# Attention output for four heads at once in column tiles of 32, and V of batch 0 begun in halves

## Chip, cores, metric

The kernel runs on one core of one Trainium2 chip. The metric is device time in microseconds of one execution. One execution is also taken by the hardware profiler, and the profile and trace below are of that one.

## What is computed

Two networks stand one behind the other. The first is attention in blocks, 4 batches of 8 heads, 768 positions in 8 blocks of 96, head size 64. A small matrix per head (8 x 8) is made doubly stochastic in five rounds; with it the blocks of K and V are mixed, and every block of Q attends to its mixed block. The second is a gated MLP with a spatial gate over the 512 columns that the heads give together.

```
for _ in range(5):
    P = exp(P - max(P)); P = P / sum(P, -1); P = P / sum(P, -2)
k_sorted = einsum('bhij,bhjcd->bhicd', P, k_b)      # the same for v
scores = scale * q_b @ k_sb.T                        # per block, 96 x 96
attn = exp(scores - max); attn = attn / sum(attn)
x = (attn @ v_sb) as (B, S, H * D)
h = relu(x @ w_in); u, v = halves of h
v_n = (v - mean) / sqrt(var + 1e-6)
v_s = w_spatial @ v_n + b_spatial
out = (u * v_s) @ w_out
```

## The kernel before

The work is cut into units, and the order of the units on TensorE, VectorE, ScalarE and GpSimd is written out by hand in one string, SCHEDULE. A unit such as `a41-2` reads: kind `a`, number 4, batch 1, no engine for the copy, PSUM slot 2; `A` and `D` name ScalarE and VectorE for the copy out of PSUM. There are four PSUM slots (tiles ps0 to ps3), each of two banks, so a unit waits until the unit that held its slot before has been read out. Every engine takes its instructions in the order in which the units stand.

The kinds are these. `k` and `q` mix and transpose K, and transpose Q (L288, L276; q unit n gives head pairs 2n and 2n+1); `v` mixes V (L246), which then goes through DRAM (vm to vd to vb, issued on SP's queue) to change its layout; for batch 0 units `t` and `B` do that with transposes instead (L288, L315). `s` makes scores of a pair of heads and half of the blocks, with one exponential on ScalarE (L331, L338). `a` (attend) makes the attention output of a pair of heads and four blocks: eight matmuls of 96 columns (L352), which write 64 partitions for each head, two matmuls with a matrix of ones for the sums of the exponentials (L359), and a Ln on ScalarE (L365). `d` (divide) ends it with an Exp of -1 times the Ln (L371) and a multiply on VectorE (L375) into xt, the transposed input of the MLP. Unit n of `s`, `a` and `d` stands for head pair n // 2 and half n % 2 of the blocks, so each batch has eight of each.

Of the MLP, `V` is the second half of the first projection with its statistics (L393, relu L227, bn_stats L407), three units a batch; `N` the normalization (L413 to L418); `U` the first half (L428); `S` the spatial product (L443) with an add on VectorE (L454) and a product with u on GpSimd (L455; on VectorE in the last batch); `O` the last projection (L465) and the store. `w` transposes w_spatial once. V, N, U, S, O of one batch are interleaved with the attention of the next.

Ahead of the units stands the sinkhorn loop on ScalarE and VectorE. Its result p_bf (32 rows of batch and head) is brought to all partitions by `spread_t` (eight matmuls, a copy) and `spread` (a matmul with a selector, a copy to prep_sb), and `make_pdiag` multiplies it with a mask. For batch 0 that is done at once; for the other three it stands in the string as `P` and `R`, just before V of batch 0, with the products on GpSimd.

Loads of q, k, v and the weights, with a cast, are issued on GpSimd's queue. Loads of batch b+2 are issued when the first S unit of batch b comes up, behind two one-element copies on GpSimd (gate, L537), which read vb of batch b+1 and so wait for its way through DRAM.

Of the kernel before, what the change touches and what calls it, by code (L numbers as in the profile page):

```python
# [8 lines left out]
FP32 = mybir.dt.float32  # L9
# [7 lines left out]
def _raw_ap(base_ap: bass.AP, off_delta: int, dims) -> bass.AP:  # L17
    return bass.AP(
        tensor=base_ap.tensor,
        offset=base_ap.offset + off_delta,  # L20
        ap=[list(d) for d in dims],
    )

# [6 lines left out]
def kernel(  # L30
# [12 lines left out]
    nc = tc.nc  # L43
# [22 lines left out]
    ex_pool = ctx.enter_context(tc.tile_pool(name="ex", bufs=7))  # L66
    xt_pool = ctx.enter_context(tc.tile_pool(name="xt", bufs=8))
    ln_pool = ctx.enter_context(tc.tile_pool(name="ln", bufs=4))
    moe_pool = ctx.enter_context(tc.tile_pool(name="moe", bufs=4))
    vs_pool = ctx.enter_context(tc.tile_pool(name="vs", bufs=2))  # L70
# [20 lines left out]
    def load_heads(x, b, name):  # L91
# [21 lines left out]
    sel16 = const.tile([8, 128], BF16)  # L113
    nc.gpsimd.memset(sel16, 0.0)
    nc.gpsimd.affine_select(
        out=sel16.rearrange("p (j t) -> p j t", t=TB),
        in_=sel16.rearrange("p (j t) -> p j t", t=TB),
        pattern=[[1, NB], [0, TB]], compare_op=ALU.not_equal,
# [6 lines left out]
    ones = const.tile([BLK, D], BF16)  # L125
# [4 lines left out]
    nc.gpsimd.dma_start(out=w_in_sb, in_=moe_w_in.rearrange("(kc p) f -> p kc f", p=128))  # L130
# [42 lines left out]


    pts = {}

    def spread_t(b, nb, ps):
        n = nb * NB * H
        t = ps_tile(ps)
        for i in range(NB):  # L180
            nc.tensor.matmul(
                t[0:NB, 0, 0:n].rearrange("p (b i h) -> p b i h", i=NB, h=H)[:, :, i, :],
                lhsT=p_bf[:, i, :], rhs=ident_bf[0:BH, b * H:(b + nb) * H],
                start=True, stop=True,
            )
        pts[b] = small.tile([NB, B * NB * H], BF16, name="pt", tag="pt", bufs=2)
        nc.vector.tensor_copy(out=pts[b][:, 0:n], in_=t[0:NB, 0, 0:n])

    def spread(b, nb, ps):
        n = nb * NB * H  # L190
        t = ps_tile(ps)
        nc.tensor.matmul(t[:, 0, 0:n], lhsT=sel16, rhs=pts[b][:, 0:n], start=True, stop=True)
        nc.vector.tensor_copy(
            out=prep_sb[:, b:b + nb].rearrange("p b i h -> p (b i h)"), in_=t[:, 0, 0:n],
        )

    pdiag = [pd_pool.tile([128, H, NB, TB], BF16, name="pdiag") for _ in range(B)]

    def make_pdiag(b, eng, h0, n):
        eng.tensor_mul(  # L200
            out=pdiag[b][:, h0:h0 + n],
            in0=_raw_ap(mask16, 0, [mask16.ap[0], [0, n], [TB, NB], [1, TB]]),
            in1=_raw_ap(prep_sb, b * NB * H + h0, [prep_sb.ap[0], [1, n], [H, NB], [0, TB]]),
        )
# [29 lines left out]
    class Attention:  # L234
        def __init__(self, b):
# [4 lines left out]
            self.xt, self.vb, self.acc, self.mixed = {}, None, {}, []  # L240
# [105 lines left out]
        def attend(self, n, eng, ps):  # L346
            hp, ih = n // 2, n % 2
            t = ps_tile(ps)
            for ii in range(NB // 2):
                for hh in range(2):  # L350
                    h, i = 2 * hp + hh, ih * (NB // 2) + ii
                    nc.tensor.matmul(  # L352
                        t[hh * 64:hh * 64 + 64, 0, ii * BLK:(ii + 1) * BLK],
                        lhsT=self.vb[:, i, h // (H // 2), h % (H // 2), :],
                        rhs=self.e[n][:, hh, ii, :],
                        start=True, stop=True,
                    )
            for hh in range(2):
                nc.tensor.matmul(  # L359
                    t[hh * 64:hh * 64 + 64, 1, 0:HW], lhsT=ones,  # L360
                    rhs=self.e[n][:, hh].rearrange("p i c -> p (i c)"),
                    start=True, stop=True,
                )
            lns = ln_pool.tile([128, HW], FP32, name="lns", tag="lns")
            nc.scalar.activation(out=lns, in_=t[:, 1, 0:HW], func=AF.Ln)  # L365
            self.acc[n] = t, lns

        def divide(self, n, eng, ps):
            hp, ih = n // 2, n % 2
            t, lns = self.acc[n]  # L370
            nc.scalar.activation(out=lns, in_=lns, func=AF.Exp, scale=-1.0)  # L371
            if hp not in self.xt:
                self.xt[hp] = xts[self.b, hp] = xt_pool.tile([128, S], BF16, name="xt", tag="xt")
            i0 = ih * (NB // 2)
            nc.vector.tensor_mul(  # L375
                out=self.xt[hp].rearrange("p (g i t) -> p i g t", g=G, i=NB)[:, i0:i0 + NB // 2],
                in0=t[:, 0, 0:HW].rearrange("p (i g t) -> p i g t", g=G, t=TB),
                in1=lns.rearrange("p (i g t) -> p i g t", g=G, t=TB),
            )


    class Gmlp:
        def __init__(self, b):
            self.b, self.last = b, b == B - 1
            self.v, self.u, self.gt, self.mv = {}, {}, {}, None
            self.xt = [xts[b, kc] for kc in range(KC)]

        def vproj(self, n, eng, ps):
            t = ps_tile(ps)
            for x in range(2):  # L390
                g = 2 * n + x
                for kc in range(KC):
                    nc.tensor.matmul(  # L393
                        t[:, x, :], lhsT=self.xt[kc][:, g * 128:(g + 1) * 128],
# [182 lines left out]
```

The softmax here doesn't subtract the row's maximum and nothing guards it: scores larger than these inputs give would overflow.

## Time and profile before

| | |
|---|---|
| median of 4 runs | 167.25 us (164.66 to 168.71) |
| the profiled execution | 168.69 us, span from first to last instruction 166.9 us |
| mean granted TensorE clock in it | 0.969 |
| TensorE matmuls busy | 152.3 us |
| ScalarE busy | 109.9 us |
| VectorE busy | 97.3 us |
| GpSimd busy | 43.1 us |
| Ln, 32 of 128 x 384 (L365) | 14.4 us, 486 ns each |
| Exp of the divide, 32 of 128 x 384 (L371) | 15.7 us, 526 ns each |
| multiply into xt, 32 of 128 x 384 (L375) | 16.9 us, 554 ns each |

Busy time of a row is the time in which at least one of its instructions is under way. Matmuls overlap one another, so their mean duration (209 ns for the eight of an attend unit) says little of what one costs; the chain of waits counts only what each adds. In the row of the granted clock (PEclk) each of the 40 digits stands for 4.2 us, 9 for full clock and 5 for half.

### The profile page before, as it was taken

Reading aid. Unit: us, or ns where it says so; the run is one execution under the profiler, and the core shown is the slowest. Engines: PE = TensorE matmul, PEld = TensorE weight load, DVE = VectorE, ACT = ScalarE, POOL = GpSimd, SP = SyncE. Lnnn points to the kernel's source line nnn. Section 1 sums busy time; section 2 is a strip of 40 time slices with the busy share of each in tenths; the row PEclk is TensorE's granted clock in tenths of the full one; section 3 lists DMA queues with packets and bytes.
Section 4 is the critical chain, followed back from the end, with each engine's and each line's share of the span. In section 5 each row is a group of like instructions: output and inputs, shape, how many; then the busy total and the mean of one; then the engine's idle time right before and its main releaser. Section 6 shows DMA issues by size and latency. Waiting matters only on the chain.

```text
span 166.9 us, 3916 instructions
## 1 busy us (share of the span) xinstructions
PE 152.3 (91%) x1645; PEld 88.2 (53%) x1645; DVE 97.3 (58%) x203; ACT 109.9 (66%) x181; POOL 43.1 (26%) x46
## 2 busy tenths in 40 slices
PE   0979996999999999999996999999999999999880
PEld 0266863546856554457663454458655544565330
DVE  4667887158971552389222255788242658849951
ACT  3168997368877777689956496489959964560041
POOL 7931000970029560000059230000163300000000
PEclk9999997599999999999999599999999999999999
DMA  2999999999657997605529993616400036000045
GB/s 15 198 204 209 231 255 186 205 204 228 221 127 95 202 204 198 251 7 168 171 46 175 204 177 132 251 57 198 126 4 0 4 132 251 0 0 4 0 184 193
DMA packets 21554, 23.86 MB, mean 143 GB/s; under 512 B 736, under 2 KB 18144, under 8 KB 21408
## 3 DMA queue, kind: packets, MB, share of 16 engines
q0 software_dynamic: 13760, 12.58, 47.1%
q1 hardware_dynamic: 7776, 11.02, 18.5%
q8 instruction: 13, 0.21, 0.5%
q14 instruction: 5, 0.04, 0.1%
HBM read 27.14 MB, written 8.65 MB: 214 GB/s over the span
## 4 chain that ended last, share of the span: by engine, by line
PE 64%; DVE 11%; ACT 10%; DMA 6%; issue 5%; POOL 2%; DVEq 0%; POOLq 0%; SPq 0%
PE ps L393 14%; PE ps L443 13%; PE ps L465 10%; PE ps L428 10%; PE ps L352 4%; ACT ex L338 3%; DVE vs L454 3%; PE ps L331 3%; PE ps L359 2%; DMA vb<-vd 2%; DVE gt L455 2%; PE ps L288 2%; PE ps L246 2%; PE ps L276 2%; PE ps L212 2%
## 5 line engine op out<-in xcount | busy, mean ns | idle before, releaser
L443 PE MATMUL ps<-wspT,v_sb 128*128 128x384 bf16 x192 | 35.1, 338 | 0.0
L338 ACT ACTIVATE ex<-ps 96x768 bf16<-96x768 f32 x32 | 24.3, 806 | 8.7 <-PE ps L331 8.6
L454 DVE TENSOR_TENSOR vs<-ps,b_bc 128x768 f32<-128x768 f32 (+1 forms) x20 | 15.9, 795 | 23.2 <-PE ps L443 18.2
L455 POOL TENSOR_TENSOR gt<-vs,u_sb 128x768 bf16<-128x768 f32 x12 | 19.7, 1653 | 34.4 <-ACT ex L338 31.4
L375 DVE TENSOR_TENSOR xt<-ps,lns 128x384 bf16<-128x384 f32 x32 | 16.9, 554 | 19.7 <-ACT lns L371 19.7
L443 PEld LDWEIGHTS <-v_sb 128*128 128x128 bf16 x192 | 18.3, 101 | 12.8 <-issue 1.9
L393 PE MATMUL ps<-w_in_sb,xt 128*128 128x512 bf16 x96 | 24.3, 407 | 0.0
L465 PE MATMUL ps<-w_out_sb,gt 128*128 128x512 bf16 x96 | 22.2, 380 | 0.8 <-DVE gt L455 0.8
L428 PE MATMUL ps<-xt,w_in_sb 128*128 128x384 bf16 x128 | 22.6, 326 | 0.0
L227 ACT ACTIVATE v_sb<-ps 128x1024 bf16<-128x1024 f32 (+1 forms) x15 | 12.5, 852 | 15.4 <-PE ps L393 15.4
L407 DVE BATCH_NORM_STATS2 stats<-v_sb 128x6 f32<-128x512 bf16 x24 | 16.3, 677 | 10.9 <-ACT v_sb L227 10.8
L428 PEld LDWEIGHTS <-w_in_sb 128*128 128x128 bf16 x128 | 12.2, 98 | 8.1
L221 ACT COPY o_sb<-ps 128x256 f32<-128x256 f32 (+1 forms) x11 | 7.3, 663 | 13.8 <-DVE o_sb L223 12.1
L365 ACT ACTIVATE lns<-ps 128x384 f32<-128x384 f32 x32 | 14.4, 486 | 2.9 <-PE ps L359 2.9
L393 PEld LDWEIGHTS <-xt 128*128 128x128 bf16 x96 | 9.8, 104 | 12.1 <-issue 2.0
L371 ACT ACTIVATE lns<-lns 128x384 f32<-128x384 f32 x32 | 15.7, 526 | 0.2
L465 PEld LDWEIGHTS <-gt 128*128 128x128 bf16 x96 | 8.6, 98 | 12.4 <-DVE gt L455 1.3
L352 PE MATMUL ps<-ex,vb 96*64 96x96 bf16 x256 | 11.3, 209 | 2.5 <-DVE vs L454 1.6
L352 PEld LDWEIGHTS <-vb 96*64 96x64 bf16 x256 | 8.6, 109 | 7.7 <-issue 6.3
L227 ACT ACTIVATE u_sb<-ps 128x768 bf16<-128x768 f32 x13 | 10.3, 809 | 1.7 <-PE ps L428 1.2
L359 PE MATMUL ps<-ex,ones 96*64 96x384 bf16 x64 | 10.8, 326 | 0.0
L221 ACT CAST kT<-ps 128x768 bf16<-128x768 f32 x13 | 10.0, 806 | 1.0 <-PE ps L288 1.0
(73 smaller groups left out, 176.8 us busy)
## 6 DMA issues: line engine op xcount, KB each, us to landing
out_dram<-o_sb SPq DMA_DIRECT2D x9, 512.0 KB, 2.8
q_in<-in_q_dram POOLq DMA_DIRECT2D x4, 768.0 KB, 10.9
k_in<-in_k_dram POOLq DMA_DIRECT2D x4, 768.0 KB, 13.9
v_in<-in_v_dram POOLq DMA_DIRECT2D x4, 768.0 KB, 10.2
vd<-vm SPq DMA_DIRECT2D x6, 384.0 KB, 3.7
vb<-vd SPq DMA_DIRECT2D x6, 384.0 KB, 3.6
out_dram<-o_sb SPq DMA_DIRECT2D x6, 256.0 KB, 2.1
wsp_nat<-in_moe_w_spatial_dram POOLq DMA_DIRECT2D x1, 1152.0 KB, 22.1
```

The costliest lines, as they stand in the source:

```text
L221: nc.scalar.copy(out=out, in_=in_)
L227: nc.scalar.activation(out=out, in_=in_, func=AF.Relu)
L338: nc.scalar.activation(out=e.rearrange("p h i c -> p h (i c)"), in_=t[0:BLK, :, 0:NB // 2 * BLK], func=AF.Exp, scale=scale,)
L352: nc.tensor.matmul(t[hh * 64:hh * 64 + 64, 0, ii * BLK:(ii + 1) * BLK], lhsT=self.vb[:, i, h // (H // 2), h % (H // 2), :], rhs=self.e[n][ ...
L375: nc.vector.tensor_mul(out=self.xt[hp].rearrange("p (g i t) -> p i g t", g=G, i=NB)[:, i0:i0 + NB // 2], in0=t[:, 0, 0:HW].rearrange("p (i ...
L393: nc.tensor.matmul(t[:, x, :], lhsT=self.xt[kc][:, g * 128:(g + 1) * 128], rhs=w_in_sb[:, kc, DH:DFF], start=(kc == 0), stop=(kc == KC - 1),)
L407: nc.vector.bn_stats(out=stats, in_=v_sb[:, x, :])
L428: nc.tensor.matmul(t[:, x, 0:HW], lhsT=w_in_sb[:, kc, mc * 128:(mc + 1) * 128], rhs=self.xt[kc][:, x * HW:(x + 1) * HW], start=(kc == 0), ...
L443: nc.tensor.matmul(t[:, x, 0:HW], lhsT=self.v[g][:, mc * 128:(mc + 1) * 128], rhs=wspT[:, g, x * HW:(x + 1) * HW], start=(g == 0), stop=(g ...
L454: nc.vector.tensor_add(out=vs[:, x], in0=t[:, x, 0:HW], in1=b2[:, x])
L455: eng.tensor_mul(out=gt2[:, x], in0=vs[:, x], in1=u2[:, x])
L465: nc.tensor.matmul(t[:, x, :], lhsT=self.gt[mc][:, g * 128:(g + 1) * 128], rhs=w_out_sb[:, mc, :], start=(mc == 0), stop=(mc == FC - 1),)
```

## The change

Attend units now serve four heads (half j of the heads) and four blocks. The head's 64 columns are taken in two halves dh of 32, and the four heads write the four groups of 32 partitions of one PSUM tile, with a tile position for each: 32 matmuls of 96 columns in a unit, in groups of four heads. The sums get a unit of their own, `z`: four matmuls of 384 columns with a matrix of ones of 32 columns, one Ln, one Exp for the four heads together. The unit `d` is gone; the attend unit ends with two multiplies, one for each dh. xt has one tile for each half of the heads; the rows of w_in are loaded in the order that fits it, in four DMAs instead of one.

Unit `X` does the first half (kc 0 and 1) of a V unit; for batch 0, X10 and X00 stand before U20, and V10 and V00 finish them after it. The order of units is new throughout. p_bf is transposed on VectorE in two pieces of 32 x 32, `spread` does eight matmuls with a selector each, and batch 0's pdiag is made straight from PSUM; the spread of the other batches stands ahead of the first K unit. The gate and the loads of batch b+2 come after the second S unit, in the order v, k, q. In the last batch only the last S unit is done in halves on VectorE; the other three are done as in the other batches, with the product on GpSimd. Buffers: ex 8 for 7, vs 3 for 2, xt 4 of twice the size for 8.

```diff
...
-    ex_pool = ctx.enter_context(tc.tile_pool(name="ex", bufs=7))
-    xt_pool = ctx.enter_context(tc.tile_pool(name="xt", bufs=8))
+    ex_pool = ctx.enter_context(tc.tile_pool(name="ex", bufs=8))
+    xt_pool = ctx.enter_context(tc.tile_pool(name="xt", bufs=4))
     ln_pool = ctx.enter_context(tc.tile_pool(name="ln", bufs=4))
...
-    vs_pool = ctx.enter_context(tc.tile_pool(name="vs", bufs=2))
+    vs_pool = ctx.enter_context(tc.tile_pool(name="vs", bufs=3))
     vsb_pool = ctx.enter_context(tc.tile_pool(name="vsb", bufs=4))
...
-    sel16 = const.tile([8, 128], BF16)
-    nc.gpsimd.memset(sel16, 0.0)
+    sel = const.tile([BH, NB // 2, 128], BF16)
+    nc.gpsimd.memset(sel, 0.0)
     nc.gpsimd.affine_select(
-        out=sel16.rearrange("p (j t) -> p j t", t=TB),
-        in_=sel16.rearrange("p (j t) -> p j t", t=TB),
-        pattern=[[1, NB], [0, TB]], compare_op=ALU.not_equal,
+        out=sel.rearrange("p i (j t) -> p i j t", t=TB),
+        in_=sel.rearrange("p i (j t) -> p i j t", t=TB),
+        pattern=[[NB, NB // 2], [1, NB], [0, TB]], compare_op=ALU.not_equal,
         fill=1.0, base=0, channel_multiplier=-1,
...
-    ones = const.tile([BLK, D], BF16)
+    DQ = D // 2
+    ones = const.tile([BLK, DQ], BF16)
     nc.vector.memset(ones, 1.0)
...
-    nc.gpsimd.dma_start(out=w_in_sb, in_=moe_w_in.rearrange("(kc p) f -> p kc f", p=128))
+    for j in range(2):
+        for dh in range(2):
+            nc.gpsimd.dma_start(
+                out=w_in_sb[:, 2 * j + dh, :],
+                in_=_raw_ap(
+                    moe_w_in, (j * (H // 2) * D + dh * DQ) * DFF,
+                    [[D * DFF, H // 2], [DFF, DQ], [1, DFF]],
+                ),
+            )
     nc.gpsimd.dma_start(out=b_nat, in_=_raw_ap(moe_b_spatial, 0, [[0, 128], [1, S]]))
...
+    pdiag = [pd_pool.tile([128, H, NB, TB], BF16, name="pdiag") for _ in range(B)]
+    def make_pdiag(b, eng, h0, n, src=None):
+        base = h0 if src is not None else b * NB * H + h0
+        src = prep_sb if src is None else src
+        eng.tensor_mul(
+            out=pdiag[b][:, h0:h0 + n],
+            in0=_raw_ap(mask16, 0, [mask16.ap[0], [0, n], [TB, NB], [1, TB]]),
+            in1=_raw_ap(src, base, [src.ap[0], [1, n], [H, NB], [0, TB]]),
+        )
+    p_t = pers.tile([BH, 2, BH], BF16)
+    def transpose_p():
+        for x in range(2):
+            nc.vector.transpose(
+                out=p_t[:, x, :], in_=p_bf[:, x * (NB // 2):(x + 1) * (NB // 2), :].rearrange("p i j -> p (i j)"),
+            )
...
+        if b:
+            nc.tensor.matmul(t[:, 1, :], lhsT=ident_bf, rhs=warm_sb, start=True, stop=True)
+        for i in range(NB):
+            nc.tensor.matmul(
+                t[:, 0, 0:n].rearrange("p (b i h) -> p b i h", i=NB, h=H)[:, :, i, :],
+                lhsT=sel[:, i % (NB // 2), :],
+                rhs=p_t[:, i // (NB // 2), b * H:(b + nb) * H],
+                start=True, stop=True,
+            )
+        if b == 0:
+            for h0, nh in ((0, 2), (2, 2), (4, 4)):
+                make_pdiag(0, DVE, h0, nh, t.rearrange("p x c -> p (x c)"))
+        else:
+            nc.vector.tensor_copy(
+                out=prep_sb[:, b:b + nb].rearrange("p b i h -> p (b i h)"), in_=t[:, 0, 0:n],
+            )
...
-            self.xt, self.vb, self.acc, self.mixed = {}, None, {}, []
+            self.xt, self.vb, self.r, self.mixed = {}, None, {}, []
...
-        def attend(self, n, eng, ps):
-            hp, ih = n // 2, n % 2
+        def sums(self, m, eng, ps):
+            j, ih = m // 2, m % 2
+            t = ps_tile(ps)
+            for c in range(H // 2):
+                nc.tensor.matmul(
+                    t[c * DQ:(c + 1) * DQ, 0, 0:HW], lhsT=ones,
+                    rhs=self.e[4 * j + 2 * (c // 2) + ih][:, c % 2].rearrange("p i c -> p (i c)"),
+                    start=True, stop=True, tile_position=(0, c * DQ),
+                )
+            lns = ln_pool.tile([128, HW], FP32, name="lns", tag="lns")
+            nc.scalar.activation(out=lns, in_=t[:, 0, 0:HW], func=AF.Ln)
+            nc.scalar.activation(out=lns, in_=lns, func=AF.Exp, scale=-1.0)
+            self.r[m] = lns
+        def attend(self, m, eng, ps):
+            j, ih = m // 2, m % 2
             t = ps_tile(ps)
...
+                i = ih * (NB // 2) + ii
+                for dh in range(2):
+                    for c in range(H // 2):
+                        nc.tensor.matmul(
+                            t[c * DQ:(c + 1) * DQ, dh, ii * BLK:(ii + 1) * BLK],
+                            lhsT=self.vb[:, i, j, c, dh * DQ:(dh + 1) * DQ],
+                            rhs=self.e[4 * j + 2 * (c // 2) + ih][:, c % 2, ii, :],
+                            start=True, stop=True, tile_position=(0, c * DQ),
+                        )
+            if j not in self.xt:
+                self.xt[j] = xts[self.b, j] = xt_pool.tile([128, 2, S], BF16, name="xt", tag="xt")
+            i0, r = ih * (NB // 2), self.r[m]
+            for dh in range(2):
+                nc.vector.tensor_mul(
+                    out=self.xt[j][:, dh, :].rearrange(
+                        "p (g i t) -> p i g t", g=G, i=NB)[:, i0:i0 + NB // 2],
+                    in0=t[:, dh, 0:HW].rearrange("p (i g t) -> p i g t", g=G, t=TB),
+                    in1=r.rearrange("p (i g t) -> p i g t", g=G, t=TB),
+                )
...
+            self.vt = {}
+        def xt(self, kc):
+            return xts[self.b, kc // 2][:, kc % 2, :]
+        def vsteps(self, n, ps, kcs):
+            if n not in self.vt:
+                self.vt[n] = ps_tile(ps)
+            for kc in kcs:
+                for x in range(2):
+                    g = 2 * n + x
                     nc.tensor.matmul(
-                        t[:, x, :], lhsT=self.xt[kc][:, g * 128:(g + 1) * 128],
+                        self.vt[n][:, x, :], lhsT=self.xt(kc)[:, g * 128:(g + 1) * 128],
                         rhs=w_in_sb[:, kc, DH:DFF],
...
                     )
+        def vstart(self, n, eng, ps):
+            self.vsteps(n, ps, range(KC // 2))
+        def vproj(self, n, eng, ps):
+            self.vsteps(n, ps, range(KC // 2 if n in self.vt else 0, KC))
+            t = self.vt[n]
             if self.mv is None:
...
-                        rhs=self.xt[kc][:, x * HW:(x + 1) * HW],
+                        rhs=self.xt(kc)[:, x * HW:(x + 1) * HW],
                         start=(kc == 0), stop=(kc == KC - 1),
...
-            if self.last:
+            final = self.last and len(self.gt) == FC - 1
+            if final:
                 pairs = [(g, x) for x in range(2) for g in range(G)]
...
-            for x in (slice(0, 1), slice(1, 2)) if self.last else (slice(0, 2),):
+            for x in (slice(0, 1), slice(1, 2)) if final else (slice(0, 2),):
                 nc.vector.tensor_add(out=vs[:, x], in0=t[:, x, 0:HW], in1=b2[:, x])
...
+        k00A2 k10D3 k20A0 s10-1 s00-2 s30-3 k30D0 t30D1 t00A2 t20D0 s20-3 s50-1 t10D2 s70-0
+        B00D3 s60-1 s40-2 B30D0 B10D3 z00-1 B20D2 z10-0 a00-1 a10-3 z20-2 a20-0 z30-1 a30-2
+        X10-3 X00-1 U20D0 V10-- V00-- w10D2 w30A0 V20-3 v01A1 U10A0 v11A3 v31D2 w00A1 U00D0
+        k01A3 v21D1 w40A2 w20D0 w50D3 k11A1 k21A2 k31A0 q11D3 q01D1 N00-- U30A2 s51-0 s71-3
+        S10-1 s31-2 s01-0 S20-3 s11-1 s21-2 S00-0 z31-3 z01-1 S30-2 s41-3 s61-0 a01-1 z11-2
+        a31-3 a11-0 z21-1 a21-2 O10A3 O00D1 O20D0 V01-2 v32A3 v02D1 V21-0 v22A2 V11-3 v12A0
+        U11A1 k32A2 q12D3 k12A0 q02D1 k02D2 N01-- k22A3 U21A0 s32-1 s22-3 S11-2 s72-0 s42-1
+        S21-3 s52-2 s02-0 U01A1 s62-3 s12-2 U31D0 z02-1 S01-3 z32-2 z12-1 S31-0 z22-2 a32-3
+        a02-1 a22-2 a12-0 O11D3 O01A1 O21A2 V02-0 v33A3 v03D1 V22-2 v23A0 V12-3 v13A2 U12A1
+        k33A0 q13D3 k13A2 q03D1 k03D0 N02-- k23A3 U22A2 s33-1 s23-3 S12-0 s73-2 s43-1 S22-3
+        s53-0 s03-2 U02A1 s63-3 s13-0 U32D2 z03-1 S02-3 z33-0 z13-1 S32-2 z23-0 a33-3 a03-1
+        a23-0 a13-2 O12D3 O02A1 O22A0 V03-2 V13-3 V23-1 N03-- U03A0 U13A2 U23A3 U33A1 S03-0
+        S13-2 S23-3 S33-1 O03A0 O13A2 O23A3
     """
...
-        "v": "vmix", "k": "ktr", "q": "qtr", "s": "score", "a": "attend", "d": "divide",
+        "v": "vmix", "k": "ktr", "q": "qtr", "s": "score", "z": "sums", "a": "attend",
         "t": "vtr", "B": "vblk",
-        "V": "vproj", "N": "norm", "U": "uproj", "S": "spatial", "O": "oproj",
+        "X": "vstart", "V": "vproj", "N": "norm", "U": "uproj", "S": "spatial", "O": "oproj",
     }
...
+        warm(2, 1)
+        transpose_p()
+        spread(0, 1, 0), spread(1, 3, 1)
+        for x in range(1, B):
+            make_pdiag(x, nc.gpsimd, 0, H)
+        nc.gpsimd.tensor_copy(
+            out=b_bc.rearrange("p (g c) -> p g c", g=G),
+            in_=b_nat.rearrange("p (c g) -> p g c", g=G),
+        )
         for step in SCHEDULE.split():
...
+            if name == "w":
                 wsp_unit(n, eng, ps)
-            elif name in "VNUSO":
+            elif name in "XVNUSO":
                 if b not in gmlp:
...
+                    eng = DVE if b == B - 1 and len(gmlp[b].gt) == FC - 1 else nc.gpsimd
                 getattr(gmlp[b], UNITS[name])(n, eng, ps)
+                if name == "S" and b + 2 < B and len(gmlp[b].gt) == 2:
+                    gate = small.tile([1, 2], BF16, name="gate", tag="gate")
+                    for x in range(2):
+                        nc.gpsimd.tensor_copy(
+                            out=gate[:, x:x + 1], in_=attn[b + 1].vb[0:1, 0, x, 0, 0:1],
+                        )
+                    v_in[b + 2] = load_heads(v, b + 2, "v_in")
+                    k_in[b + 2] = load_heads(k, b + 2, "k_in")
+                    q_in[b + 2] = load_heads(q, b + 2, "q_in")
             else:
```

## Prediction

> **What bounds the kernel now.** First the page: engine shares, granted clock by slice, the chain's shares.
>
> ```profile
> PE 152.3 (91%) x1645; PEld 88.2 (53%) x1645; DVE 97.3 (58%) x203; ACT 109.9 (66%) x181; POOL 43.1 (26%) x46
> PEclk9999997599999999999999599999999999999999
> PE 64%; DVE 11%; ACT 10%; DMA 6%; issue 5%; POOL 2%; DVEq 0%; POOLq 0%; SPq 0%
> ```
>
> TensorE is the bound on average, and its clock is halved twice. ScalarE's 66% is worth something only where it leads. So next the chain in order of time:
>
> ```profile
> 22.09 0.41 ACT lns L371
> 22.50 0.39 ACT lns L365
> 22.91 0.52 ACT lns L371
> ...
> 26.46 0.53 ACT lns L371
> 27.01 0.56 DVE xt L375
> 27.57 0.27 DVE pt L187
> 27.88 0.34 PE ps L192
> 28.21 3.52 PE ps L393 x8
> ```
>
> Until 28.2 us batch 0 hangs on ScalarE: score exponentials, then a Ln and an Exp per attention unit. The first eight V matmuls then take 3.52 us; eight later ones take 1.73 (216 ns for 512 columns, 0.42 ns per column). The half rate lasts to about 34. From 28 to 148 TensorE runs without a gap, but for one place in batch 2, in the timelines of GpSimd and TensorE:
>
> ```profile
> 84.83 0.18 POOL L537 COPY gate<-vb 1x1 bf16<-1x1 bf16 x1 [4.32 <-DMA vb<-vd]
> 88.04 4.87 POOL L455 TENSOR_TENSOR gt<-vs,u_sb 128x768 bf16<-128x768 f32 x3
> 90.77 0.36 PE L352 MATMUL ps<-ex,vb 96*64 96x96 bf16 x8 [1.60 <-DVE vs L454]
> 91.87 3.80 PE L443 MATMUL ps<-wspT,v_sb 128*128 128x384 bf16 x12
> ```
>
> GpSimd's gate copies wait for V's trip through DRAM; the gate products stand behind them, the two vs buffers stay full, VectorE waits, TensorE idles 1.6 us. The S unit after it runs at half rate: 3.73 us in the chain where the others take 2.06.
>
> The attention units, from the chain:
>
> ```profile
> 130.46 0.36 PE ps L352 x8
> 130.82 0.16 PE ps L359 x2
> 130.99 1.87 PE ps L465 x8
> 132.86 0.29 PE ps L352 x8
> 133.15 0.16 PE ps L359 x2
> 133.31 0.17 PE ps L352 x8
> ```
>
> Eight matmuls of 96 columns in 0.17 us are 21 ns each, though one streams 96 x 0.42 = 40 ns: the two tiles of 64 columns run side by side. Two sums of 384 columns take 0.16, the time of one. A unit after another kind of matmul pays about 0.12 more (0.29 against 0.17). In batch 3 the eight units took 0.79 + 0.79 + 0.53 + 1.23 = 3.34 us.
>
> The tail, TensorE's timeline and the landing of q_in:
>
> ```profile
> 157.94 4.06 PE L465 MATMUL ps<-w_out_sb,gt 128*128 128x512 bf16 x18 [0.81 <-DVE gt L455]
> DMA to landing us min/median/max: 7.4/10.9/31.4
> ```
>
> In the tail VectorE's eight pairs of add and product pace the end. The 31.4 is q_in of batch 1, issued at 9.1 on GpSimd's queue, landed at 40.5; the loads of that queue land one after the other, 3.9 us for each head tensor (v_in of batch 1 at 32.7, k_in at 36.6).
>
> [...]
>
> **The front (to V of batch 0).** Removed: spread_t, its copy, the second spread with the 0.27 + 0.34 us just before V. Added: two VectorE transposes, eight selector matmuls per spread, pdiag of batch 0 straight from PSUM. p_bf stands at 11.23. Mask copy 0.2; two transposes are unknown: nearest row, a 32x64 multiply at 0.21, so 0.4 (0.3 to 0.8); eight matmuls 0.34 as L181's. First pdiag at about 12.4 instead of 12.60. Three pdiag pieces at L200's prices (0.43, 0.43, 0.69) instead of 0.43 and 0.95, plus the other batches' prep copy 0.35 moved here: the first K copy starts about where it did (13.7).
> ScalarE then: two K copies and the wait between them to 15.5, eight exponentials at 0.70 back to back (2.11 for three), one V copy 0.75, and instead of eight Ln/Exp pairs of 0.9 four: 15.5 + 5.6 + 0.75 + 3.6 = 25.5, where it ended at 28.2. Now VectorE is late next: from 12.4, pdiag 1.55, prep 0.35, five copies of 0.92, four vb copies of 0.67, eight xt multiplies of 0.51 = 13.2, and 1.7 of waiting on slots (the last K copy for ScalarE, B30 for ex70): 27.3. V need not wait for that: X10 takes slot 3, free after the second multiply of a10, the fourth of the eight: about 25.4. X10 and X00, eight matmuls, lie beside the multiplies of a20 and a30; U20's second half finds xt at 27.3. V begins 2.8 us earlier: **-2.8** (0 if VectorE's waits double, -3.5 if transposes cost nothing).
> The half clock costs 2.9 us now (28.2 to 34). [...] Whether that keeps the clock is open: 0 to -2.9. At full clock TensorE reaches q11 at 39.8 and waits for q_in at 40.5, which caps the gain. I take **-1.0**. The same cap holds for v01 (32.5 against 32.7) and k01 (36.5 against 36.6). Splitting w_in into four issues adds about 1.6 us of issuing on GpSimd, and the ninth and later loads wait for older ones, but the queue is backlogged until 43, so nothing lands later. pdiag of batches 1 to 3 moves from 28 to about 20 on GpSimd, covered: v01 reads it after 32.
> In the V stage, w10, v21 and w20 now copy on VectorE behind the bn_stats of three V units; TensorE waits for slots at v21, w20, k11: **+0.7**.
>
> **Attention in batches 1 to 3.** Removed per batch: 3.34 us of units. Added: four sums (z), four tiles of 32 at once, 0.16 each; four attends of 32 matmuls. Four at a time that is 8 x 42 ns = 0.34, as much array time as two old units; three switches at 0.12. Together 0.64 + 1.36 + 0.36 = 2.36: **-1.0 per batch, -3.0 in all**. Not shown: four tiles at once. Bounds: 0.34 (all overlap) and 0.68 (21 ns per matmul, two at a time); I take 0.34, because starts that lie this close show no per-instruction cost.
> ScalarE saves 16 pairs, 16 x (0.486 + 0.526) = 16 us, 12 of them in these batches: off the path, so nothing. VectorE's 32 multiplies stay. But an attend now holds a slot until two multiplies are through, and z needs a slot until its Ln: stepping through the order, I find O11 waiting 0.5 for slot 3 (a32's multiplies behind the add of S31), and 0.1 to 0.3 at z11, a11, a22: **+0.7 per batch, +2.1** (0 to 4).
>
> **The gate.** It moves behind the second S unit; vs has three buffers; all four V mixes come before U. In batch 2 the last mix (v12) is then 10.7 us of TensorE work ahead of the end of S21, plus 2.6 for its add and product; the trip took about 9 (mixed at 75.9, landed at 84.8). So no wait on it: **-1.6 - 1.7 = -3.3** (0 to -3.3). The three loads are issued later: in batch 0 at about 51.5 instead of 49.7. v_in then lands at about 60 and v32 asks at 62.7; k_in before q_in now, at 63.7 and 67.6, asked at 68.1 and 68.5. Covered, by 1 us at the least; if the cover goes, TensorE waits for what is missing.
>
> **The tail.** Three of the four S units go to VectorE's add (0.96) and GpSimd's product (1.65), each under the 2.06 of an S unit. From the start of S03: S23's product on GpSimd ends at 8.9, S33's halves on VectorE at 8.45 and 9.55, so O03 goes on at 9.0 where it now goes on at 157.94 - 147.86 = 10.1: **-1.1** (0 to -1.5).
>
> **Sum.** -2.8 - 1.0 + 0.7 - 3.0 + 2.1 - 3.3 - 1.1 = -8.4 against the profiled execution, 168.7 (span 166.9 and 1.8 around it): **160.3**, with a span of about 158.5. That execution lies 1.4 above the median of 167.25; executions with fewer half-rate windows will stand lower on both sides.
>
> **Rivals.**
> Early gain lost to loads and slots (0.16): q_in on its serial queue and VectorE's longer list take the 3.8 of the front and clock, slots 1 more: about 165. For it: 0.7 us of slack at q_in. Against: U20 and two k units, 2 us, are done before q11 that came after it.
> Four tiles two at a time (0.10): 12 x (0.34 + 0.16) = 6.0 more: 166.3, no change.
> Slower (0.06): tiles of 32 don't overlap. An attend is 32 x 42 = 1.36, a z 0.64: 12 x (1.02 + 0.48) = 18: 178. It decides once an attend and its z take over 0.50 + 8.4/12 = 1.2 us. Against it: the pairs of today.
> Clock kept as well (0.08): no early half-rate window, q_in capping it: about 158.
> My forecast has 0.60, its own range 158 to 163. Measurement of this kernel tells about 2% from no change. Faster 0.79 (forecast, clock kept, and about half of the 165 case whose lower end lies under 163.9), same 0.14, slower 0.07. Range 156.5 to 166, with the two-at-a-time case at its upper edge.
>
> **What would show it.** Right: attend units of 32 matmuls in 0.3 to 0.4 us of chain; V begun at 25 to 26 behind an xt multiply; no idle at the gate and S01 at 2.06; ScalarE near 94 us; O03 resuming 9 us after S03. Wrong: attends of 0.7 or more, TensorE idle at L276 on q_in, GpSimd's gate before a wait of TensorE, or half rate in places where it is full now.

## The result, and the profile after

The changed kernel takes as long as the one before: 167.28 us in the median of 43 runs (164.47 to 170.55) against 165.83 in 64 runs of the kernel before beside them, a ratio of 1.0005 [0.9984, 1.0025]. The forecast of 160.3 lies under every run. Executions of both kernels differ in how much half clock they hold (mean granted clock 0.967 to 1.000 before, 0.949 to 0.989 after); the ratio leaves the longest ones out, but both profiled executions (168.7 and 170.55 us) are among these, so what is read from them is held against the traces of other kernels below.

The page of the changed kernel: engine shares, granted clock by slice, the chain's shares, and the line of queue q8, whose kind it calls "instruction" (packets, MB, share of the DMA engines).

```profile
span 168.8 us, 4366 instructions
PE 148.7 (88%) x1897; PEld 86.4 (51%) x1897; DVE 98.7 (58%) x201; ACT 91.9 (54%) x142; POOL 50.3 (30%) x52
PEclk9999997599999996599999999999999999999997
PE 72%; DMA 8%; DVE 8%; issue 5%; ACT 3%; POOL 2%; POOLq 1%; DVEq 0%
q8 instruction: 15, 0.25, 0.6%
```

TensorE has 3.6 us less to do and ScalarE 18 us less (109.9 to 91.9, foreseen near 94), yet the span is 1.9 us longer: the saved time has become idle time. Half rate has moved: the stretch around 92 is gone, one at 64.7 to 71.5 is new. The chain in order of time shows where the idle time is (start, length, what; "issue" is a wait for nothing that the profile shows):

```profile
24.07 0.68 PE ps L387 x64
24.75 0.17 PE ps L369 x4
24.92 0.08 PE ps L387 x6
25.00 3.59 issue
28.59 0.74 PE ps L387 x25
...
61.80 0.16 PE ps L369 x4
61.96 0.32 PE ps L387 x29
62.27 3.19 issue
65.47 0.27 PE ps L387 x3
65.73 8.15 PE ps L501 x24
```

Two attend units are cut in the middle of their 32 matmuls, for 3.59 and 3.19 us. The profile names no semaphore, slot or load that ends these waits. After the second the clock falls, and the 24 O matmuls take 8.15 us where they take 5.34 in batch 2. There is one more wait in the front, in TensorE's timeline:

```profile
17.74 1.20 PE L307 MATMUL ps<-pdiag,v_in 128*64 128x128 bf16 x36 [1.77 <-DMA v_in<-in_v_dram]
```

v_in of batch 0 landed at 16.3 before and at 17.7 after, and everything behind it on GpSimd's queue of loads (the software queue below) is late: the four pieces of w_in come at 24.9 to 25.6 (22.0 before), v_in of batch 1 at 36.4 (32.7), its q_in at 44.2 (40.5). GpSimd issued this q_in only at 25.2 us (9.1 before), when the first piece of w_in had landed.

Batch 2 and the tail went as worked out:

```profile
99.58 0.28 PE ps L369 x4
99.85 0.71 PE ps L387 x64
100.56 1.02 DVE xt L397 x2
101.58 0.14 issue
101.72 5.34 PE ps L501 x24
...
150.60 5.86 PE ps L479 x36
...
159.37 1.68 PE ps L501 x7
```

Stage by stage, from the first V matmul of a batch (its end is the start of the next):

| stage | before | after | difference | forecast |
|---|---|---|---|---|
| start to end of O of batch 0 | 66.9 | 73.9 | +7.0 | -3.4 |
| attention of batch 2, to the end of O of batch 1 | 37.0 | 33.2 | -3.8 | -3.6 |
| attention of batch 3, to the end of O of batch 2 | 33.7 | 33.2 | -0.5 | -0.3 |
| tail, from V of batch 3 | 29.3 | 28.6 | -0.7 | -1.1 |

(The forecast's first row is front, clock, V stage and the attention of batch 1.) The whole miss, 10.4 us, is in the first row. Three things there that the forecast lacks make 11.4: two stalls 6.8, half rate on O 2.8, the v_in wait 1.8. They are not independent of one another, and the half clock at 27 to 34, which the forecast hoped to shorten, stayed too, so this is no exact account.

### The profile page after: what moved, and what is told of

Read it like the earlier page. It is cut to its first block, busy times and chain, and to the rows that moved or that the text cites. A ratio compares the mean times of both kernels' runs of the same rounds, so it can differ in the third digit from the quotient of the medians.

```text
span 168.8 us, 4366 instructions
## 1 busy us (share of the span) xinstructions
PE 148.7 (88%) x1897; PEld 86.4 (51%) x1897; DVE 98.7 (58%) x201; ACT 91.9 (54%) x142; POOL 50.3 (30%) x52
## 2 busy tenths in 40 slices
DMA packets 23139, 23.89 MB, mean 142 GB/s; under 512 B 2320, under 2 KB 19728, under 8 KB 22992
## 3 DMA queue, kind: packets, MB, share of 16 engines
q0 software_dynamic: 15344, 12.59, 50.0%
## 4 chain that ended last, share of the span: by engine, by line
PE 72%; DMA 8%; DVE 8%; issue 5%; ACT 3%; POOL 2%; POOLq 1%; DVEq 0%
PE ps L479 18%; PE ps L501 14%; PE ps L420 12%; PE ps L463 11%; DMA v_in<-in_v_dram 8%; PE ps L350 4%; PE ps L307 3%; PE ps L387 3%; PE ps L295 2%; DVE stats L442 2%; PE ps L369 2%; ACT ex L357 2%; PE ps L265 2%; DVE xt L397 1%; DVE vm L242 1%
## 5 line engine op out<-in xcount | busy, mean ns | idle before, releaser
L491 POOL TENSOR_TENSOR gt<-vs,u_sb 128x768 bf16<-128x768 f32 x15 | 24.6, 1647 | 94.6 <-ACT ex L357 67.4
L479 PE MATMUL ps<-wspT,v_sb 128*128 128x384 bf16 x192 | 33.4, 327 | 0.0
L501 PE MATMUL ps<-w_out_sb,gt 128*128 128x512 bf16 x96 | 24.4, 415 | 0.9 <-DVE xt L397 0.8
L463 PE MATMUL ps<-xt,w_in_sb 128*128 128x384 bf16 x128 | 23.2, 328 | 0.0
L442 DVE BATCH_NORM_STATS2 stats<-v_sb 128x6 f32<-128x512 bf16 x24 | 16.2, 675 | 11.4 <-ACT v_sb L246 11.4
L240 ACT COPY o_sb<-ps 128x256 f32<-128x256 f32 (+1 forms) x11 | 7.3, 664 | 28.3 <-PE ps L501 16.5
L397 DVE TENSOR_TENSOR xt<-ps,lns 128x384 bf16<-128x384 f32 x32 | 15.5, 549 | 5.8 <-PE ps L387 5.5
L501 PEld LDWEIGHTS <-gt 128*128 128x128 bf16 x96 | 9.7, 105 | 14.2 <-issue 4.9
L420 PEld LDWEIGHTS <-xt 128*128 128x128 bf16 x96 | 9.6, 101 | 11.4 <-issue 1.7
L387 PE MATMUL ps<-ex,vb 96*32 96x96 bf16 x512 | 8.3, 215 | 6.9 <-issue 6.8
L375 ACT ACTIVATE lns<-ps 128x384 f32<-128x384 f32 x16 | 7.8, 485 | 8.2 <-PE ps L369 8.2
L242 DVE COPY o_sb<-ps 128x256 f32<-128x256 f32 (+1 forms) x10 | 7.4, 742 | 7.8 <-PE ps L501 6.4
L387 PEld LDWEIGHTS <-vb 96*32 96x32 bf16 x512 | 7.4, 101 | 7.7 <-issue 7.3
L350 PEld LDWEIGHTS <-kT 64*96 64x96 bf16 x256 | 7.2, 121 | 4.6 <-issue 3.6
```

The lines of the kernel that those rows point to most:

```text
L240: nc.scalar.copy(out=out, in_=in_)
L387: nc.tensor.matmul(t[c * DQ:(c + 1) * DQ, dh, ii * BLK:(ii + 1) * BLK], lhsT=self.vb[:, i, j, c, dh * DQ:(dh + 1) * DQ], rhs=self.e[4 * j ...
L397: nc.vector.tensor_mul(out=self.xt[j][:, dh, :].rearrange("p (g i t) -> p i g t", g=G, i=NB)[:, i0:i0 + NB // 2], in0=t[:, dh, 0:HW].rearr ...
L420: nc.tensor.matmul(self.vt[n][:, x, :], lhsT=self.xt(kc)[:, g * 128:(g + 1) * 128], rhs=w_in_sb[:, kc, DH:DFF], start=(kc == 0), stop=(kc ...
L442: nc.vector.bn_stats(out=stats, in_=v_sb[:, x, :])
L463: nc.tensor.matmul(t[:, x, 0:HW], lhsT=w_in_sb[:, kc, mc * 128:(mc + 1) * 128], rhs=self.xt(kc)[:, x * HW:(x + 1) * HW], start=(kc == 0), ...
```

## The experiments

**Theory F (fetch).** F takes TensorE's instructions to come in blocks, one with each packet of q8, by these counts from the traces: each of q8's packets has 16,384 bytes; 15 of them go with 3806 records of TensorE here (matmuls, weight loads and its few semaphore instructions), 13 with 3298 before, two packets more for 508 records. The stalls stand behind records 705 and 1729, 1024 apart, and those of the runs below behind 705, 961, 1729 and 2753: 256 is the largest number that divides all these distances. So a block is taken as 256 records, an estimate from these counts. New attend code has 64 records in 0.35 us of array time, so it uses up a block in a few microseconds: the block ending at 705 was entered at 20.7 and used up by 25.0. Its successor's packet started only at 26.3, 5.6 us after that entry; the second stall's 3.1 us after. While loads of the software queue run, the other packets of this trace start 2.8 to 3.8 us after the entry; where none run, from 2.4 before it to 1.4 after. So F says: the fetch of the next block waits behind the loads, and fast code reaches the block's end first. Rivals of F: a stall that belongs to the attend code itself (tile positions, slots), and loads that come late by the split of w_in alone. The expectations below name these theories as they stood before each run.

**Shift the code against the blocks** (32 tiny matmuls, 64 instructions, after the warm-up; then 64 of them):

```diff
+    def pad(n, ps):
+        t = ps_tile(ps)
+        for _ in range(n):
+            nc.tensor.matmul(t[0:8, 0, 0:8], lhsT=ident_bf[0:32, 0:8], rhs=warm_sb[0:32, 0:8], start=True, stop=True)
...
+        pad(32, 1)
```

> 32 tiny matmuls (64 instructions with their weight loads, about 0.8 us) are put where TensorE waits for the sinkhorn loop; all other work is as in the changed kernel. Theory F (fetch): TensorE's instructions come in blocks of 256, fetched by DMA, and the two stalls stand where a block ends that was used up before the next had come. Then both stalls move by 64 instructions, 32 matmuls earlier in the order of units: the first from the 7th matmul of a20 to about the 10th of a10, the second from the 30th of a21 to about z21; the first is 2 to 4 us, the second 1.5 to 3. Rival P (place): the stalls belong to the units (a tile mode, a semaphore, a bank of PSUM): they stay in a20 and a21 at 3.6 and 3.2 us. Rival C (clock): the stalls are incidental and the time is lost to half-rate windows alone: no statement on places, time unchanged.

Measured: 165.05, ratio 0.9941 [0.9914, 0.9968], profiled span 162.3. The expectation had both stalls move; they are gone, and no other has come. That fits F, though it was not foreseen: the block that ends at record 705 now lasts 6.4 us, and the block that ends at 1729 has its successor's packet 0.9 us before it is itself entered, ahead of the loads. v_in is waited for longer, 3.48 us.

> As e1_pad64 with 64 tiny matmuls (128 instructions, 1.6 us beside the sinkhorn loop). F: the block ends then fall on the 11th matmul of a00 and on the first matmuls after X10 or V10 in the front, and on a11 in batch 1. The block before a11 then holds an S unit and lasts over 5.5 us, so the second stall is gone or under 1 us and the clock after it stays full: some 4 to 6 us less in the profile, about 164 to 166. In the front one stall of 1 to 4 us remains at one of the two places. P: stalls in a20 and a21 as before, time as the changed kernel.

Measured: 171.13, ratio 1.0324 [1.0191, 1.0457], span 168.8. The expected time, 164 to 166, was missed by far, as were the number and the lengths of the stalls: the second one is gone as expected, but three new ones have come, at block ends in other places. Two of them in TensorE's timeline, the second in a V unit, where no tile of 32 columns is:

```profile
27.92 0.77 PE L395 MATMUL ps<-ex,vb 96*32 96x96 bf16 x54 [1.26 <-issue]
33.88 0.59 PE L428 MATMUL ps<-w_in_sb,xt 128*128 128x512 bf16 x1 [2.83 <-issue]
```

They are at records 705 and 961, both block ends; a third of 1.27 us is in O at 2753, a block end too. v_in is waited for 2.72 us, and half rate holds from 19.8 to 23.2 and from 30.1 to 36.9. The code did not change but by the tiny matmuls at the start, so a stall of the attend code itself is out.

**Take the loads away.** The loads of q, k and v for batches 2 and 3, which run during the second stall, are dropped, and these batches compute on the data of batches 0 and 1; the front is untouched.

```diff
-                    v_in[b + 2] = load_heads(v, b + 2, "v_in")
-                    k_in[b + 2] = load_heads(k, b + 2, "k_in")
-                    q_in[b + 2] = load_heads(q, b + 2, "q_in")
+                    v_in[b + 2], k_in[b + 2], q_in[b + 2] = v_in[b], k_in[b], q_in[b]
```

> The loads of q, k, v for batches 2 and 3 are left out (these batches work on the data of batches 0 and 1); nothing else changes, so block ends stay where they are. F with its second half (a fetch takes 3 to 6 us only because the software queue's loads stand in its way): the first stall stays at 3.6 us, the second goes (under 0.5 us), and so does the half rate after it; 5 to 6 us less in the profile. If a fetch takes that long by itself, the second stall stays at about 3 us. P: both stay.

Measured: 164.15, ratio 0.9898 [0.9808, 0.9988]. Timeline of TensorE at the two places:

```profile
27.77 0.75 PE L387 MATMUL ps<-ex,vb 96*32 96x96 bf16 x26 [3.32 <-issue]
...
60.88 0.53 PE L387 MATMUL ps<-ex,vb 96*32 96x96 bf16 x32
61.59 4.69 PE L501 MATMUL ps<-w_out_sb,gt 128*128 128x512 bf16 x21 [0.18 <-PE ps L387]
```

The first stall stays, the second and its half clock are gone, and the block's packet starts 0.3 us before its entry instead of 3.1 after it. So for the second stall both parts of F are shown: it needs the block's end and the loads. For the first the loads can't be dropped, as the front computes on them; that part is carried over, not shown. The 1% is not the price of the second stall alone: whatever else the loads cost goes with them.

**Load w_in in one DMA again**, the rows paired so that it fits the new order:

```diff
-    for j in range(2):
-        for dh in range(2):
-            nc.gpsimd.dma_start(out=w_in_sb[:, 2 * j + dh, :], in_=_raw_ap(...))
+    nc.gpsimd.dma_start(
+        out=w_in_sb.rearrange("p (j x) f -> p j (x f)", j=2),
+        in_=_raw_ap(moe_w_in, 0, [[2 * DFF, 128], [(H // 2) * D * DFF, 2], [1, 2 * DFF]]),
+    )
...
-                            lhsT=self.vb[:, i, j, c, dh * DQ:(dh + 1) * DQ],
+                            lhsT=self.vb[:, i, j, c, :].rearrange("p (d x) -> p x d", x=2)[:, dh, :],
```

> w_in in one DMA again: even and odd columns of a head instead of first and second half, so that a partition reads two neighbouring rows of 8 KB in all; the attend's weights are then read with a step of two. If the four DMAs with an outer dimension of 4 are what slowed the queue, v_in of batch 0 lands at 16.3 instead of 17.7, w_in at about 22 instead of 25.6, q_in of batch 1 at 40.5 instead of 44.2, and 1.4 us of waiting at t30 go. F: the first stall stays in a20, perhaps shorter, since less stands in the fetch's way; time 1 to 2 us less. If the order of loads on the queue and not the form of the DMA was the cause: nothing changes. If weights with a step of two load slower, attends go from 0.35 to over 0.5 us.

Measured: 164.32, ratio 0.9857 [0.9633, 1.008], by itself unclear. Its timeline isn't:

```profile
16.36 1.36 PE L302 MATMUL ps<-pdiag,v_in 128*64 128x128 bf16 x36 [0.36 <-DMA v_in<-in_v_dram]
25.30 0.48 PE L382 MATMUL ps<-ex,vb 96*32 96x96 bf16 x26 [1.71 <-issue]
60.15 0.22 PE L382 MATMUL ps<-ex,vb 96*32 96x96 bf16 x3 [2.04 <-issue]
```

w_in lands at about 21.9, 15.6 us after its issue; the four pieces took 17.3 to 18.6. That repeats: in the four traces with pieces the last lands at 25.4 to 26.2, in the ten with one DMA w_in lands at 21.9 to 22.2, and while the pieces move, in the fifth and sixth of the page's 40 slices, the core's DMA moves 134 to 151 GB/s where it moves 213 to 273 with one. The stalls stay at the same two records, at a half and two thirds of their length, and half rate follows the second here too (60.9 to 64.3): the rival "late by the split alone" is out, and the split and the fetch are two costs. Why four pieces are slower was not shown. One difference stands in the pages: in the changed kernel's the software queue has 15344 packets, in this kernel's 13504, and packets under 512 B are 2320 against 736; whether that is the cause was not tried.

The wait for v_in of batch 0 is not so clearly the split's. With pieces v_in lands at 16.5 (without the loads), 17.7, 19.3 and 19.4. With one DMA it lands at 16.2 or 16.3 in the four kernels without tiny matmuls, but at 17.1 to 17.3 in the six with them, which follow below. In these six a packet of q8 starts at 14.1 to 15.2, ahead of the landing, in those four at 16.8 to 17.4, behind it. That a fetch holds up a load in its turn would explain it, but was not tested.

**Both together**, the one DMA with 32 and with 64 tiny matmuls, and those 32 in the kernel before as a control:

> w_in in one DMA (as e4_win) and 64 instructions ahead of the first spread (as e1_pad64) together. F: neither the wait for v_in at t30 nor the two stalls at block ends, and no half rate after the second stall. From e4_win's span of 162.3: less 1.7 and 2.0 for its stalls, less 1.7 for the half-rate window after the second: span about 157, time 158 to 160, which is the sum that the prediction made (160.3). If the pads helped e1_pad64 only by chance of the clock: 162 to 164, with stalls in a20 and a21.

> e5_win_pad64 with 64 tiny matmuls ahead of the first spread instead of 32, that is block ends 64 instructions earlier in the order of units. F: a stall comes back in the front, at TensorE's record 705 or 961 (in a00, or at V10 after X and U20, the block between them being used up in 3 to 5 us), 0.5 to 3 us, perhaps with a half-rate window after it: 162 to 166. If only the number of instructions or the load of w_in mattered: as e5, 161.

> The kernel before with the same 32 tiny matmuls ahead of its first spread (64 instructions, beside the sinkhorn loop). F: the kernel before has no stall at a block end over 0.5 us, so there is nothing to take away: within 1 percent of the kernel before, or up to 1 us slower where a block end now meets an attend unit. If the tiny matmuls themselves help, by keeping TensorE's clock up in the front or otherwise, and not by where block ends fall: 1.7 to 3.4 us faster, and e5's gain is not the change's.

Measured: 160.93 with 32, ratio 0.9698 [0.965, 0.9746], span 158.8; 168.7 with 64, ratio 1.0113 [1.0035, 1.0191]; the control 167.22, ratio 1.0044 [1.0016, 1.0072]. The kernel with 32: clock by slice in the profiled execution, TensorE's wait for v_in of batch 0, its first V unit, and two transfers of its chain, q_in of batches 1 and 2:

```profile
PEclk9999999999999999999999999999999999999999
```

```profile
17.32 1.20 PE L310 MATMUL ps<-pdiag,v_in 128*64 128x128 bf16 x36 [1.32 <-DMA v_in<-in_v_dram]
25.98 1.89 PE L423 MATMUL ps<-w_in_sb,xt 128*128 128x512 bf16 x7 [0.24 <-DVE xt L400]
```

```profile
9.91 30.91 DMA q_in<-in_q_dram
40.86 1.53 PE ps L298 x48
...
53.93 17.98 DMA q_in<-in_q_dram
```

And TensorE's timeline of the kernel with 64:

```profile
29.35 3.14 PE L423 MATMUL ps<-w_in_sb,xt 128*128 128x512 bf16 x7 [3.04 <-issue]
```

The two kernels compute the same from the same loads and differ by 64 instructions; 7.8 us lie between them (4.2% by the ratios, some 7 us). The stall shown is at a block end again (record 961), one of 1.95 us follows at the block end 2753, and half rate holds from 29.4 to 32.8. The expectation, 162 to 166, had the first stall but not the second. The control says that the tiny matmuls don't help by themselves; they cost 0.4%. By these ratios the whole way from the changed kernel to 160.93 is 3.1% (5.1 us): of it the single w_in gives 1.5% alone (with an interval of over 2% on either side) and 2.4% on top of the shift, the shift 0.6% alone and 1.6% on top of w_in (a step that lies within the interval of the single w_in). That is less than the 6.8 us of stalls in the profiled execution; why, is open, as only that execution of the changed kernel has a trace.

**Parts of the change tried one by one.** The gate and the loads ahead of the first S unit, in the order v, q, k, as before (in the kernel of 160.93):

```diff
-                getattr(gmlp[b], UNITS[name])(n, eng, ps)
-                if name == "S" and b + 2 < B and len(gmlp[b].gt) == 2:
+                if name == "S" and b + 2 < B and not gmlp[b].gt:
...
+                getattr(gmlp[b], UNITS[name])(n, eng, ps)
```

> e5_win_pad64 with the gate and the loads of batch b+2 ahead of the first S unit, in the order v, q, k, as before the change. Prediction's step: the later gate is worth up to 3.3 us in the old order of units. Here V's mixes come earlier, so if their place is what took the wait away, the early gate costs 0 to 1 us; if the gate's place is, TensorE idles again before or after an S unit and 2 to 3 us come back. The loads then start 2 to 5 us earlier and may stand in the way of another fetch: a stall at a block end (TensorE's records 193 + n x 256) would show that.

Measured: 162.3, ratio 0.979 [0.9708, 0.9871]. One wait of 1.53 us comes back, at 55.5 in the attention of batch 1, and none in that of batch 2. The medians differ by 1.4 us, but the two intervals overlap, so what the gate's place is worth isn't separated; batch 2's wait is gone whatever the place, which leaves the earlier V mixes (they were not tried alone). After the first S unit instead of the second (2 to 1 in the condition) is the best version:

> e5_win_pad64 with the gate and the loads of batch b+2 behind the first S unit instead of the second (order v, k, q as there). In e5 q_in of batch 2 lands late and TensorE waits 1.3 us for it; ahead of the first S unit (e6) that wait is gone, but TensorE waits 1.5 us in the attends of batch 1. If the loads' start is what counts: about 2 us earlier, no wait for q_in, and the gate has just been passed: 159.5 to 160.3. If the gate at this place holds the products of S20 and S00 as in e6: 160.9 to 162.3.

Measured: 160.24, ratio 0.9643 [0.9578, 0.9709]. q_in of batch 2 no longer makes TensorE wait (1.3 us at 71 in the kernel of 160.93). The 0.7 us between the two versions are not separated: their intervals overlap.

Without the half V units X (V10, V00 whole, ahead of U20):

> e5_win_pad64 with V of batch 0 in one piece: V10 and V00 stand whole ahead of U20, no X. V10's second half then waits for the second half of xt, so eight matmuls of 512 columns (1.7 us at full clock) no longer lie beside the multiplies of a20 and a30: 1 to 2 us more, up to 3.5 if that idle time brings a half-rate window more. If VectorE's chain does not lead there, nothing.

Measured: 162.2, ratio 0.9768 [0.9714, 0.9822], 1.3 us more, with intervals that overlap a little. A gap of 2.06 us has come, behind record 953:

```profile
33.81 0.49 PE L234 MATMUL ps<-ident_bf,wsp_nat 128*128 128x128 bf16 x6 [2.06 <-DVE u_sb L251]
```

It lies near a block end, 961, but is no fetch: the packet of the block behind 961 ended at 28.2, and what ends the gap is VectorE's copy of u, which stands behind the statistics of the V units. So the gap belongs to the order without X, and X is worth 1.3 us by the medians.

The kernel before with the tail alone changed (only the last S unit in halves):

> The kernel before with the tail's part of the change alone: in the last batch only the last S unit in halves with its product on VectorE, the other three with the product on GpSimd. Prediction's step: O03 goes on 9.0 us after the start of S03 instead of 10.1, 1.1 us less in all. If two matmuls more behind the wait and the copies' chain take it back, as the changed kernel's tail (28.6 against 29.3 us) suggests: 0.6 us less. If GpSimd's last product is late: nothing.

Measured: 165.69, ratio 0.9975 [0.9939, 1.0011]; from the first add of the last batch to the end 16.82 becomes 16.12 us in the profiles. The 0.7 is too small for the times.

The kernel before with each attend matmul split into two of 32 columns:

```diff
-                    nc.tensor.matmul(t[hh * 64:hh * 64 + 64, ...], lhsT=self.vb[..., :], rhs=..., start=True, stop=True)
+                    for dh in range(2):
+                        r0 = hh * 64 + dh * 32
+                        nc.tensor.matmul(t[r0:r0 + 32, ...], lhsT=self.vb[..., dh * 32:dh * 32 + 32], rhs=..., start=True, stop=True, tile_position=(0, r0))
```

> The kernel before with each attend matmul split into two of 32 columns (two halves of d, tile positions 0, 32, 64, 96): 16 instead of 8 matmuls in a unit, same PSUM layout, sums, Ln, Exp and order of units; 512 instructions more on TensorE, as many as the change brings. F: the units stand apart (a Ln and an Exp between them in the front, S and O units later), so a block of 256 lasts over 5 us nearly everywhere: no stall over 1 us and the time of the kernel before within 1 percent; units of 16 at 0.17 us as units of 8 before. If the number of instructions itself costs (a rate of issue): 256 matmuls more at 10 to 20 ns, 2.5 to 5 us slower. If tiles of 32 don't run four at a time: 0.34 us a unit, 5 us slower.

Measured: 172.86, ratio 1.0386 [1.0326, 1.0446]: the expectation fell, in the time and in the stall. Its chain:

```profile
56.04 0.28 PE ps L354 x16
56.32 0.28 PE ps L361 x2
56.61 0.28 PE ps L354 x16
56.89 0.28 PE ps L361 x2
```

Sixteen matmuls of 32 columns would take the array time of eight of 64 (0.16, an estimate: 0.28 less the change), but every change between tiles of 32 and sums of 64 columns now costs 0.12 (two sums take 0.28, in the kernel before 0.16): 0.57 us for a unit against 0.42 (3.34 / 8), 1.2 us a batch. Beside this there is a stall of 1.43 at record 705 again, where the expectation had none over 1 us (it had the block last over 5 us; it was used up in 4.8), and half rate from 25.9 to 36.1; what each has of its 6 us was not priced apart. The change escapes these switches since its sums have 32 columns as well (0.16 to 0.17 for four sums between two attends).

## Why the prediction was wrong, point by point

- **The step that failed: instruction fetch, put at nothing.** The working took the attend unit at array time because starts that close "show no per-instruction cost". As a rate that held; it says nothing of 256 instructions being used up in 4.3 us while loads run. In the profiled execution this is +6.8 and the half rate on O +2.8 (both come again, shorter, in the kernel with one w_in); in the comparisons 0.6 to 1.6%. In before's trace no block end has a gap over 0.3 us; in the changed kernel's two have 3.6 and 3.2 us.
- **"Nothing lands later" failed.** Splitting w_in was charged 1.6 us of issuing, covered. The pieces themselves are slower: w_in was there some 3.6 us later, and v_in, k_in and q_in of batch 1 behind it 3.6 to 3.7. GpSimd's issues of these three waited for older loads, 2.5 us for k_in of batch 0, 4.4 for its v_in and 6.4 for the first piece; before, only the issue of w_out did, 2.8 us for k_in. (v_in of batch 0, 1.4 us later and waited for 1.8, varies too much between the traces to be put down to the split.) The one-DMA versions are 1.5 and 2.4% faster. The rival "early gain lost to loads and slots" (165) had the right end of the kernel, but named neither cost.
- **Front, -2.8: nearly right where stalls and split are gone.** V begins at 25.98 behind an xt multiply, foreseen 25.4, although TensorE still waits 1.32 us for v_in; with them it begins at 30.29, where it began at 28.21.
- **Half clock, -1.0 (the author's estimate), with q_in as a cap at 40.5:** in the changed kernel it is not gained; with both costs gone the clock stays full in the profiled execution, and TensorE waits for q_in until 40.8. That is the rival "clock kept", whose cap was right.
- **Attention, -1.0 + 0.7 a batch: right.** 64 matmuls take 0.68 to 0.71, so an attend 0.34 to 0.35: four tiles at once, and "two at a time" and "don't overlap" fall. Batch 3 gives -0.5 for -0.3.
- **Gate, -3.3: right for the profiled execution.** No idle time at it and no half rate near 92; the stage of batch 2 gives -3.8 for -3.6. But the 1.7 us of half rate in it were not there in every execution: in the control, the kernel before with 32 tiny matmuls, TensorE waits 2.3 us at the same place and the clock stays full behind it. And the loads, "covered, by 1 us at the least", were not: with both costs gone q_in of batch 2 lands at 71.9, not 67.6, and TensorE waits 1.3 us for it.
- **Tail, -1.1: mis-sized.** O goes on 8.8 us after the last S units begin, as worked out (9.0). But it is paced at its end by the output copies on VectorE and ScalarE, 0.42 and 0.37 each, one after the other; -0.7 is left.
- **Absolute against relative.** With both missing costs gone the kernel runs at 160.93 and its span is 158.8, where 160.3 and 158.5 were forecast. Against the kernel before that is 3.0% or 5 us, not the 8.4 of the sum: this was made against a profiled execution that lies 2.9 above the median of 165.83, so that 160.93 comes so near to 160.3 is in part luck. The chances of the prediction are off by a little as well: 0.60, 0.08 and half of 0.16 are 0.76, not 0.79.

## What to carry to other kernels

Before many small instructions are put in place of few, count them against the 256 records that a block had here, and ask whether loads run while a block is used up in less than about 5 us. In the traces of all the kernels here there were ten such blocks, and each ended in a stall of 1.3 to 3.6 us; one that lasted 7.1 us did too. Blocks that were used up as fast, but whose next packet came while no loads ran, ended in no gap over 0.4 us. If a wait called "issue" appears in the middle of a uniform group of matmuls, count records from the stall to the next one. Treat a time at one alignment as one draw: 64 instructions at the start moved the one-DMA kernel from 160.9 to 168.7. A DMA that is split is to be priced by its landing and by every transfer behind it on the queue, not by its issue: here four issues took 2.7 us where one took 0.8, and landings came 3.6 us later.

## What the runs showed of the hardware

- The packet of a TensorE instruction block mostly takes about 1 us (0.9 to 1.7 in the changed kernel's trace), but it began up to 5.7 us after the previous block was entered while software-queue loads ran, and at most 2.2 us after it, often before it, where none did; at all eleven stalls TensorE went on 1.3 to 1.6 us after the packet's end. By what the loads make the packet wait was not tried.
- Four column tiles of 32 let matmuls with their weight loads start 11 ns apart (64 in 0.71 us in the changed kernel), against 21 for two tiles of 64 (8 in 0.17 us before).
- Changing between column tiles of 32 and of 64 cost 0.12 us (two sums took 0.28 in the kernel before with split attends, 0.16 without the split), as much as changing from full tiles (eight attend matmuls 0.29 against 0.17 before).
- At the end of one idle stretch of 3.2 us in the changed kernel the granted clock fell to half for 6.8 us, and the 24 O matmuls behind it took 8.15 us, 2.8 more than in batch 2. One stretch of 2.0 us (one w_in) was followed by half rate as well, one of 2.3 us (the control) was not; what decides it was not shown.
